# Attention and squared-ReLU MoE kernel: chunk 1's strided heads on TensorE, the first chunk's heads in another order, and gh written by VectorE in chunk 0

## Chip, cores and metric

The kernel runs on one core of one Trainium2 chip. The metric is the device time of one execution in microseconds. Three runs of the kernel before took 883.71 to 884.16 us, the median is 883.96 us. Its engines are named as the profile does: PE (TensorE, matmuls), PEld (its weight loads), DVE (VectorE), ACT (ScalarE), POOL (GpSimd) and SP (SyncE, which issues the DMAs).

## The reference

Attention over 8 batches, 8 heads, 576 positions and head size 64, with two masks: heads 0 to 3 are local (each position sees itself and the 31 before it), heads 4 to 7 are strided (each position sees those before it with the same remainder by 32). The result, as 4608 tokens of 512 features, goes through a feed-forward layer of width 2048 with a squared ReLU.

```python
scores = scale * np.matmul(q, k.transpose(0, 1, 3, 2))
mask_local = (rel >= 0) & (rel < stride)
mask_strided = (rel >= 0) & (pos[None, :] % stride == pos[:, None] % stride)
...
attn = attn / (np.sum(attn, axis=-1, keepdims=True) + 1e-09)
out = np.matmul(attn, v)
...
h = np.maximum(x @ w_in, 0.0)
return (h * h @ w_out).astype(np.float32)
```

## The kernel before

**Chunks and slots.** The tokens are cut into 12 chunks of 384 (`SEGS` names the two pieces of 192 of each). For each chunk, 16 slots j go over the 2048 features, 128 at a time. `up` (L452) makes 12 matmuls of 128x384 into a PSUM tile h: four pieces of x (two local ones, `xlh`/`xll` for their high and low part, two strided ones, `xsh`/`xsl`), each as high x high, high x low and low x high. ScalarE and VectorE then square the ReLU and split it into `gh` and `gl`, and `down` (L480) makes nine matmuls of 128x512 per slot into three y tiles. An up slot of a chunk needs all four pieces of its x.

**Attention.** Where the heads of a chunk are computed depends on the chunk. Chunk 0 takes all its heads through TensorE, in pairs (`pe_pair`, L292): two local pairs (`first`) and two strided pairs (`late`), whose positions are sorted by remainder so that the mask is block-wise. A pair is loaded (q and k in one tile `qk`, v in another), then come scores on TensorE with masked minima on VectorE, exponentials and normalising (factor `rs`), transposes on TensorE with copies to `pt`, and output matmuls, whose results are split into x's high and low part. Chunk 1 takes its local pairs this way too (`local`, L540), in chunk 0's slots. Its strided heads, and those of all later chunks, are computed by `strided` (L387) on GpSimd and VectorE: products per lane on GpSimd (L412 tile `pq`, L434 tile `pp`), each reduced by VectorE (L413, L435). The local heads of chunks 2 to 11 go through `pe_head` (L196).

**The buffers around the seam.** In chunk 1 all matmuls of a pair go to one PSUM bank, number 3, in turn: `pair_at(c, pr, True, pr, "3")`. In chunk 0 each pair has two banks of its own. A pair's SBUF tiles are taken from pools that are used in rotation; the second pair's v and both its score tiles come from the pool of three y output tiles (`ysb`).

**Weights.** They arrive as 64-bit integers' halves and are converted by `convert` (L147): ScalarE scales the raw tile (L154) and makes z (L166), VectorE joins them (L169), ScalarE casts the high part (L172), GpSimd subtracts for the low part (L173). Three of 16 tiles are converted before the first slot, the others in chunk 0's slots.

**The order.** In chunk 0, `up` and `down` of each slot are written one after the other, down two slots behind up. From slot 16 on, slots go in twos: two ups, two downs, with the next chunk's `pe_head` steps between, and each group is fixed behind the one before it. So chunk 1's first two up slots are followed by chunk 0's down slots 14 and 15. Between these fixed groups a scheduler places everything else, by readiness in its own model; `SPREAD` sets how fast the steps for chunk 1 are handed to it in chunk 0's slots (11 slots for the local pairs, 8 for the strided heads). Each engine, SP's DMA issues among them, then works through its queue in the written order.

Of the kernel before, what the change touches and what calls it, by code (L numbers as in the profile page):

```python
# [12 lines left out]
ALU = mybir.AluOpType  # L13
# [28 lines left out]

SPREAD = ((11, 8), (13, 13))

# [42 lines left out]
def attn_moe(ctx: ExitStack, tc, qk_l, v_l, qk_d, v_d, qk_p, v_p, f_s, q_s, k_s, v_s, w_in, w_out, masks, eye, out):  # L87
# [59 lines left out]
    def convert():  # L147

        split = None

        def scale(k):
            for raw, _ in raws[k]:

                nc.scalar.activation(f32(raw[:, :, 1]), f32(raw[:, :, 1]), AF.Prelu, scale=2.0**-112, alpha=-(2.0**32))  # L154

        scale(0)
        for k in range(NFT):
            p, which = order[k]
            t = wpool.tile([P, 2, 1024], F32R, name=f"w{which}_{p}", tag=f"w{k}")
            (wo if which else wi)[p] = t[:, 0], t[:, 1]  # L160
            cuts = [(raw[:, i : i + WP], sl.start + i) for raw, sl in raws.pop(k) for i in range(0, sl.stop - sl.start, WP)]
            for raw, at in cuts:

                z = psum(zbank[next(zturn) % len(zbank)], f"z{k}_{at}").bitcast(U32)
                w, hi, lo = raw[:, :, 1], t[:, 0, at : at + WP], t[:, 1, at : at + WP]
                first_step = nc.scalar.activation(z, raw[:, :, 0], AF.Copy, bias=-0.49, scale=2.0**-29 * (1 - 2.0**-9))  # L166
                if split:
                    split()
                last["v"] = nc.vector.scalar_tensor_tensor(out=w, in0=w, scalar=3, in1=z, op0=ALU.logical_shift_left, op1=ALU.bitwise_or)  # L169

                def split(w=w, hi=hi, lo=lo, at=at, k=k):
                    last["a"] = nc.scalar.copy(hi, f32(w))  # L172
                    last["g"] = nc.gpsimd.tensor_sub(lo, f32(w), f32(hi))  # L173
                    if at and 4 <= k < 12:
                        fetch(k + 4)

                if not at and k + 1 < NFT and k + 1 in raws:
                    with tc.issue_after(first_step.ins):
                        scale(k + 1)
                yield  # L180
        split()
# [110 lines left out]
    def pe_pair(c, pr, local, qk, vr, es, pt, banks, sm, single):  # L292
# [3 lines left out]
        if local:  # L296
            kw, wins, nv = KW, [at for _, _, at in windows(c)], P
            src, vsrc = qk_d[c, pr], v_d[c, pr]
            mk = [mask_sb[:QC, w % 2, :] for w in range(NW)]
        else:  # L300
            kw, wins, nv = QC, [QC * w for w in range(NW)], QC
            src, vsrc = qk_p[pr], v_p[pr]
            mk = [mask_sb[:QC, 3, :QC]] * NW
# [11 lines left out]
        s_ps = [banks() for _ in range(2)] if c == 0 else None  # L315
        e4 = [e[:QC, : NW * kw].rearrange("p (w k) -> p w k", k=kw) for e in es]
        def scores(h, w, s):
# [24 lines left out]
        for h in range(2):  # L342
            if single:
                for w in range(NW):
                    last["a"] = nc.scalar.activation(e4[h][:, w], e4[h][:, w], AF.Exp, bias=nm[:QC, h, w : w + 1], scale=-1.0, accum_out=ss[:QC, NW * h + w, :1])  # L345
            else:
# [5 lines left out]
        for h in range(2):  # L352
            last["g"] = nc.gpsimd.tensor_mul(e4[h], e4[h], rs[:QC, h].unsqueeze(2).broadcast_to([QC, NW, kw]))
        yield
        p4 = pt.rearrange("p (h w q) -> p h w q", h=2, w=NW)
        for h in range(2):
            t = s_ps[h] if s_ps else banks()
            for w in range(NW):
                nc.tensor.transpose(t[:kw, w * QC : (w + 1) * QC], e4[h][:, w], ident[:QC, :QC])  # L359
            last["a"] = nc.scalar.copy(pt[:kw, h * TC : (h + 1) * TC], t[:kw, :TC])  # L360
        yield
        x = x_tiles(c)
        if local:
            o = s_ps[0] if s_ps else banks()
            for w in range(NW):
                for h in range(2):
                    nc.tensor.matmul(o[D * h : D * (h + 1), w * QC : (w + 1) * QC], v4[:kw, h, w], p4[:kw, h, w], start=True, stop=True)
            outs = [(o[:, :TC], [x["l", s][:, pr, :] for s in "hl"])]
        else:

            r0 = D * pr
            outs = []
            for a in range(2):
                o = s_ps[a]
                for w in range(NW):
# [3 lines left out]
                by_i = lambda t: t[r0 : r0 + D].rearrange("p (s i r) -> p s i r", s=2, r=STR)  # L379
                outs.append((o[r0 : r0 + D, :TC].rearrange("p (s r i) -> p s i r", s=2, i=SI), [by_i(x["s", s][:, a, :]) for s in "hl"]))  # L380
        for src, (xh, xl) in outs:
            last["a"] = nc.scalar.copy(xh, src)
            last["v"] = nc.vector.tensor_sub(xl, src, f32(xh))  # L383
        yield
# [67 lines left out]
    def up(c, j):  # L452
# [14 lines left out]
        if c == 0:  # L467

            r = p_t[j % 2].rearrange("p w q -> p (w q)")
            nc.scalar.activation(r, g, AF.Relu)  # L470
            nc.vector.scalar_tensor_tensor(out=g, in0=g, scalar=0.0, in1=r, op0=ALU.max, op1=ALU.mult)
# [3 lines left out]
        last["gh"] = nc.scalar.copy(gh, g)  # L475
        nc.vector.tensor_sub(gl, g, f32(gh))  # L476
# [126 lines left out]
    with tc.issue_after(last["p"].ins):  # L603
        zeros(0, NWARM // 2)
        for k in range(NEARLY, 8):
            fetch(k)
    next(late[0])
    with tc.issue_after(last["p"].ins):
        zeros(1, NWARM // 2)
    next(first[0])  # L610
    next(first[1])
    weights = behind({"a": last["a"]}, ungated)
    next(late[1])
    for i in range(2):
        next(first[0])
        next(first[1])
        next(late[0])
        next(late[1])
        if i:
            weights = behind({"a": last["a"]}, ungated)  # L620
        for _ in range(2):
            next(weights)
    next(late[0])
    next(late[1])
    for _ in range(2 * NEARLY - 4):
        next(weights)
# [4 lines left out]
    for s in range(NS + 2):  # L631
# [29 lines left out]
        if c + 1 < NCHUNK and s >= LATER:  # L661
            j0 = LATER if c == 0 else 0
            if j == j0:
                lo, st = local(c + 1) if c == 0 else iter(()), strided(c + 1)
                if c == 0:
                    lo, st = behind(heads_end, lo), behind(heads_end, st)
                if c == 1:
# [19 lines left out]
def _layout(q, k, v, moe_w_in, moe_w_out):  # L687
# [21 lines left out]

    by_r = lambda t: rows(t[:, HL:], 0).reshape(HL, 2, SI, STR, D).transpose(0, 1, 3, 2, 4).reshape(HL, TC, D)  # L710
    a["qk_p"] = asc(np.concatenate([by_r(t).transpose(0, 2, 1) for t in (q, k)], axis=2)).reshape(2, P, 2 * TC)
    a["v_p"] = two(by_r(v).reshape(HL, NW, QC, D).transpose(0, 2, 1, 3).reshape(1, HL, QC, NW * D)).reshape(2, QC, 2 * NW * D)

# [44 lines left out]
```

## Time and profile before

| what | value |
|---|---|
| median of three runs | 883.96 us |
| the profiled execution | 883.18 us |
| its span, first to last instruction | 881.4 us |
| mean granted TensorE clock | 0.997 |
| VectorE, ScalarE, GpSimd busy | 72%, 65%, 77% |
| TensorE, PEld busy | 99%, 90% |

Columns of the profile's rows: in a timeline, start, length, engine, line, operation, output<-input, shape and count, and in brackets the idle time before and what ended it. In the chain of work that ended last, start, length, engine, tile and line; each row there is work, or a wait, that nothing else hides. In groups, the busy time of all, the mean length of one in ns, and the idle time before them with what ended it. In the table of stretches, from:to, length, busy time of each engine with its number of instructions, then the granted clock (1.00 is full), the DMA engines' busy share and GB/s. Lengths of neighbouring instructions can overlap, and one fp32 matmul counts as two records. In DMA rows, the size, and the median time from issue to landing.

### The profile page before, as it was taken

What the parts mean: (1) busy time and instruction counts of PE and PEld (TensorE: products, weight loads), DVE (VectorE), ACT (ScalarE), POOL (GpSimd) and SP (SyncE); (2) the same over time, 40 slices, a digit from 0 to 9 for tenths busy, and PEclk for the clock granted to TensorE, in tenths of its full rate; (3) what the DMA queues carried; (4) which work ended last, traced back from release to release, by engine and by line L of the source; (5) the groups of instructions that cost most, each with busy time, mean ns of one, the idle gap of its engine ahead of it and who ended that gap; (6) DMA issues with size and microseconds to landing.
All of it is one profiled execution on the core that took longest, in us unless ns stands there. A gap on an engine that the chain in (4) does not pass through costs nothing.

```text
span 881.4 us, 14862 instructions
## 1 busy us (share of the span) xinstructions
PE 868.5 (99%) x4744; PEld 789.6 (90%) x4744; DVE 635.5 (72%) x1892; ACT 572.6 (65%) x1510; POOL 676.8 (77%) x722
## 2 busy tenths in 40 slices
PE   8899999999999999999999999999999999999997
PEld 7788899999999999999999999999999989998996
DVE  4578687788777888878778778778787787883111
ACT  6798776676676666757657747657666665664332
POOL 4698878878978989898988978997898899782000
PEclk9999999999999999999999999999999999999999
DMA  9851631323123123104102302312131121000000
GB/s 356 355 195 63 184 121 42 103 84 113 32 66 112 37 89 103 44 30 127 44 13 80 115 14 74 104 31 74 31 102 57 30 71 61 7 1 10 28 1 36
DMA packets 26798, 71.41 MB, mean 81 GB/s; under 512 B 2976, under 2 KB 8736, under 8 KB 25184
## 3 DMA queue, kind: packets, MB, share of 16 engines
q1 hardware_dynamic: 26432, 70.14, 23.9%
q8 instruction: 37, 0.61, 0.3%
q10 hardware_dynamic: 288, 0.33, 0.1%
q14 instruction: 41, 0.34, 0.1%
HBM read 61.01 MB, written 9.44 MB: 80 GB/s over the span
## 4 chain that ended last, share of the span: by engine, by line
PE 95%; ACT 3%; DVE 1%; POOL 0%; issue 0%; DVEq 0%; POOLq 0%; ACTq 0%
PE h L462 44%; PE y L489 44%; PE s L234 2%; PE o L280 2%; ACT e L345 1%; PE w_ps L586 1%; ACT raw L154 1%; PE b L319 1%; DVE sc L419 0%; ACT z L166 0%; ACT w L172 0%; DVE raw L169 0%; ACT pt L360 0%; PE b L359 0%; DVE xsl L383 0%
## 5 line engine op out<-in xcount | busy, mean ns | idle before, releaser
L489 PE MATMUL y<-w,gh 128*128 128x512 f32 x1152 | 357.1, 391 | 0.8 <-ACT gh L475 0.8
L489 PEld LDWEIGHTS y<-w,gh 128*128 128x128 f32 x1152 | 212.5, 188 | 41.5 <-ACT gh L475 1.4
L462 PE MATMUL h<-xlh,w 128*128 128x384 f32 x768 | 229.6, 339 | 2.1 <-DVE xsl L383 1.6
L462 PE MATMUL h<-xsh,w 128*128 128x384 f32 x768 | 226.2, 335 | 0.0
L489 PE MATMUL y<-w,gl 128*128 128x512 f32 x576 | 224.0, 392 | 0.0
L434 POOL TENSOR_TENSOR pp<-vs,sc 128x448 f32<-128x448 f32 (+10 forms) x192 | 189.8, 1014 | 39.8 <-DVE qs L435 18.2
L412 POOL TENSOR_TENSOR pq<-ks,qs 128x512 f32<-128x512 f32 (+2 forms) x192 | 197.8, 1050 | 17.9 <-DVE sc L413 13.8
L476 DVE TENSOR_TENSOR gl<-h,gh 128x384 fp32r<-128x384 f32 x192 | 105.4, 550 | 84.2 <-ACT gh L475 82.9
L475 ACT CAST gh<-h 128x384 fp32r<-128x384 f32 x192 | 91.4, 477 | 103.0 <-PE y L489 100.0
L473 ACT ACTIVATE h<-h 128x384 f32<-128x384 f32 x176 | 83.0, 472 | 107.8 <-PE h L462 106.2
L413 DVE TENSOR_REDUCE sc<-pq 128x8 f32<-128x512 f32 (+4 forms) x228 | 119.6, 534 | 46.2 <-POOL pq L412 43.9
L462 PEld LDWEIGHTS h<-xlh,w 128*128 128x128 f32 x768 | 142.1, 188 | 5.6 <-DVE xsl L383 1.8
L462 PEld LDWEIGHTS h<-xsh,w 128*128 128x128 f32 x768 | 141.7, 188 | 0.3
L462 PE MATMUL h<-xll,w 128*128 128x384 f32 x384 | 129.3, 337 | 0.0
L435 DVE TENSOR_REDUCE qs<-pp 128x64 f32<-128x448 f32 (+11 forms) x192 | 106.7, 563 | 31.0 <-POOL pp L434 29.5
L489 PEld LDWEIGHTS y<-w,gl 128*128 128x128 f32 x576 | 108.1, 188 | 22.9
L462 PE MATMUL h<-xsl,w 128*128 128x384 f32 x384 | 128.5, 335 | 0.0
L474 ACT ACTIVATE h<-h 128x384 f32<-128x384 f32 x176 | 83.2, 473 | 3.6
L259 DVE STREAM_TRANSPOSE p_t<-e 32x128 f32<-32x128 f32 x240 | 72.3, 301 | 10.4 <-ACT e L248 6.0
L462 PEld LDWEIGHTS h<-xll,w 128*128 128x128 f32 x384 | 72.5, 189 | 2.2
L462 PEld LDWEIGHTS h<-xsl,w 128*128 128x128 f32 x384 | 72.2, 188 | 0.0
L243 ACT ACTIVATE e<-e,nm 96x128 f32<-96x128 f32 x160 | 62.5, 392 | 10.5 <-DVE nm L226 8.8
(97 smaller groups left out, 1077.2 us busy)
## 6 DMA issues: line engine op xcount, KB each, us to landing
qk<-qk_l SPq DMA_DIRECT2D x24, 400.0 KB, 3.2
y<-ysb SPq DMA_DIRECT2D x36, 256.0 KB, 3.7
raw<-w_in SPq DMA_DIRECT2D x7, 1024.0 KB, 11.2
qk<-qk_l SPq DMA_DIRECT2D x16, 416.0 KB, 3.3
vs<-v_s SPq DMA_DIRECT2D x10, 576.0 KB, 4.0
raw<-w_out SPq DMA_DIRECT2D x5, 1024.0 KB, 12.9
v<-v_l SPq DMA_DIRECT2D x40, 128.0 KB, 2.0
ks<-k_s SPq DMA_DIRECT2D x8, 576.0 KB, 3.8
```

The costliest lines, as they stand in the source:

```text
L243: nc.scalar.activation(e[:QC, cut(w)], e[:QC, cut(w)], AF.Exp, bias=nmax[:QC, w : w + 1], scale=-1.0, accum_out=ssum[:QC, w, :1])
L259: nc.vector.transpose(out=pt[STR * k : STR * (k + 1), :, STR * r : STR * (r + 1)], in_=e.rearrange("p (w k) -> p w k", k=KW)[STR * r : STR ...
L412: nc.gpsimd.tensor_mul(pv, kt[:, a : a + m, :], qt[:, i - i0 : i - i0 + 1, :].broadcast_to([P, m, D]))
L413: nc.vector.tensor_reduce(out=sc[:, i - i0, a : a + m], in_=pv, op=ALU.add, axis=AX.X)
L434: nc.gpsimd.tensor_mul(pv, vt[:, a : a + nd, :n], sc[:, il : il + 1, :n].broadcast_to([P, nd, n]))
L435: nc.vector.tensor_reduce(out=ot[:, il, a : a + nd], in_=pv, op=ALU.add, axis=AX.X)
L462: done = nc.tensor.matmul(ph[:, :TC], w[:, wsl], xx, start=n == 0, stop=n == 11)
L473: nc.scalar.activation(g, g, AF.Relu)
L474: nc.scalar.activation(g, g, AF.Square)
L475: last["gh"] = nc.scalar.copy(gh, g)
L476: nc.vector.tensor_sub(gl, g, f32(gh))
L489: done = nc.tensor.matmul(y_ps[c][t], g[:, sl], w[:, wsl], start=j == 0 and k == 0, stop=j == NFT - 1 and k == 2)
```

## The change

There are four parts.

1. **Chunk 1's strided heads** are computed by `pe_pair` on TensorE. `pairs` takes the place of `local`: after the ten steps of the two local pairs come ten steps of two strided pairs, in the same bank 3 and from the same pools, handed out over 12 slots. `strided` begins with chunk 2. The host lays out `qk_p` and `v_p` for two chunks.
2. **The first chunk's heads.** In the local pairs of chunk 0 the exponentials are written to the PSUM tile of the scores, and VectorE multiplies them with `rs` into SBUF, where GpSimd did it in place. The copies of the strided pairs' transposes to `pt` go from ScalarE to VectorE. Each output's cast and subtraction follow its matmuls at once. The steps are written in another order; 20 warm-up matmuls take the place of two times 30, and the first weight tile's second half is split at once.
3. **In chunk 0's slots** the ReLU is written twice by ScalarE, VectorE writes the product once to `gh` and once to PSUM, and ScalarE's cast to `gh` goes.
4. **`SPREAD`** becomes `((12, 8), (13, 13))`, with 20 steps where there were 10.

```diff
-SPREAD = ((11, 8), (13, 13))
+SPREAD = ((12, 8), (13, 13))
...
+                if k == 0 and at:
+                    split()
+                    split = None
...
+        r4 = [blocks(t) for t in s_ps] if single else e4
...
-                    last["a"] = nc.scalar.activation(e4[h][:, w], e4[h][:, w], AF.Exp, bias=nm[:QC, h, w : w + 1], scale=-1.0, accum_out=ss[:QC, NW * h + w, :1])
+                    last["a"] = nc.scalar.activation(r4[h][:, w], e4[h][:, w], AF.Exp, bias=nm[:QC, h, w : w + 1], scale=-1.0, accum_out=ss[:QC, NW * h + w, :1])
...
-            last["g"] = nc.gpsimd.tensor_mul(e4[h], e4[h], rs[:QC, h].unsqueeze(2).broadcast_to([QC, NW, kw]))
+            eng, key = (nc.vector, "v") if single else (nc.gpsimd, "g")
+            last[key] = eng.tensor_mul(e4[h], r4[h], rs[:QC, h].unsqueeze(2).broadcast_to([QC, NW, kw]))
...
-            last["a"] = nc.scalar.copy(pt[:kw, h * TC : (h + 1) * TC], t[:kw, :TC])
+            (nc.vector.tensor_copy if c == 0 and not local else nc.scalar.copy)(pt[:kw, h * TC : (h + 1) * TC], t[:kw, :TC])
...
+        def parts(src, dst):
+            last["a"] = nc.scalar.copy(dst[0], src)
+            last["v"] = nc.vector.tensor_sub(dst[1], src, f32(dst[0]))
...
-                o = s_ps[a]
+                o = s_ps[a] if s_ps else banks()
...
             nc.scalar.activation(r, g, AF.Relu)
-            nc.vector.scalar_tensor_tensor(out=g, in0=g, scalar=0.0, in1=r, op0=ALU.max, op1=ALU.mult)
+            last["gh"] = nc.scalar.activation(r, g, AF.Relu)
+            for t in (gh, g):
+                nc.vector.scalar_tensor_tensor(out=t, in0=g, scalar=0.0, in1=r, op0=ALU.max, op1=ALU.mult)
...
-    def local(c):
-        heads = [pair_at(c, pr, True, pr, "3") for pr in range(2)]
-        for h in (0, 0, 1, 0, 1, 0, 0, 1, 1, 1):
-            next(heads[h])
-            yield
+    def pairs(c):
+        for kind in (True, False):
+            heads = [pair_at(c, pr, kind, pr, "3") for pr in range(2)]
+            for h in (0, 0, 1, 0, 1, 0, 0, 1, 1, 1):
+                next(heads[h])
+                yield
...
-                lo, st = local(c + 1) if c == 0 else iter(()), strided(c + 1)
...
+                lo, st = (behind(heads_end, pairs(c + 1)), iter(())) if c == 0 else (iter(()), strided(c + 1))
...
-            while dl < fl * 10 and next(lo, "end") != "end":
+            while dl < fl * 20 and next(lo, "end") != "end":
```

What this does to the written order shows at the seam between chunk 0 and chunk 1. The first engine is TensorE. Before, chunk 0's down slot 13 (the rows with y) is followed by chunk 1's first up slot, h_0; the names xl are local pieces of x, xs strided ones.

```order
L489 MATMUL y_2_614<-w_6_1218,gl_13_1307 128x512
L462 MATMUL h_0_1397<-xlh_901,w_0_413 128x384
L462 MATMUL h_0_1397<-xll_902,w_0_413 128x384
L462 MATMUL h_0_1397<-xlh_901,w_0_413 128x384 x2
L462 MATMUL h_0_1397<-xll_902,w_0_413 128x384
L462 MATMUL h_0_1397<-xlh_901,w_0_413 128x384
L462 MATMUL h_0_1397<-xsh_903,w_0_413 128x384
```

Now, at the same place and behind three matmuls each for h_0 and h_1, stand the last steps of local pair 1 (b_1_1: transposes L366, outputs L379) and then the scores of the strided pairs (L325; b_0_0 is pair 0, b_1_0 is pair 1).

```order
L366 MATMUL b_1_1_926<-ident,e_1_1_651 128x96 x4
L379 MATMUL b_1_1_978<-pt_1_1_652,v_1_1_649 64x96 x8
L470 MATMUL h_0_1408<-xlh_850,w_0_372 128x384
L470 MATMUL h_1_1427<-xlh_850,w_0_372 128x384
L325 MATMUL b_0_0_1049<-qk_0_0_1035 96x96 x4
L470 MATMUL h_0_1408<-xll_851,w_0_372 128x384
L470 MATMUL h_0_1408<-xlh_850,w_0_372 128x384
L470 MATMUL h_1_1427<-xll_851,w_0_372 128x384
L470 MATMUL h_1_1427<-xlh_850,w_0_372 128x384
L325 MATMUL b_0_0_1058<-qk_0_0_1035 96x96 x4
L325 MATMUL b_1_0_1165<-qk_1_0_1040 96x96 x4
L325 MATMUL b_1_0_1174<-qk_1_0_1040 96x96 x4
```

Right behind these come the strided pairs' transposes (L366) and outputs (L389), and the rest of h_0 and h_1, which reads xs.

```order
L366 MATMUL b_0_0_1223<-ident,e_0_0_1037 96x96 x4
L366 MATMUL b_0_0_1229<-ident,e_0_0_1038 96x96 x4
L389 MATMUL b_0_0_1235<-pt_0_0_1039,v_0_0_1036 32x96 x8
L389 MATMUL b_0_0_1246<-pt_0_0_1039,v_0_0_1036 32x96 x8
L366 MATMUL b_1_0_1298<-ident,e_1_0_1042 96x96 x4
L366 MATMUL b_1_0_1304<-ident,e_1_0_1043 96x96 x4
L389 MATMUL b_1_0_1355<-pt_1_0_1044,v_1_0_1041 32x96 x8
L470 MATMUL h_0_1408<-xsh_852,w_0_372 128x384
L470 MATMUL h_1_1427<-xsh_852,w_0_372 128x384
L389 MATMUL b_1_0_1366<-pt_1_0_1044,v_1_0_1041 32x96 x8
```

So all of the strided pairs' matmuls have come to stand between two parts of chunk 1's first two up slots.

The second engine is SP, with its DMA issues for the same place. Before, the loads for chunk 2's strided heads (qkvs_4 and the rows with 6) follow the last weight tiles (raw).

```order
L144 DMA raw_512_1099<-w_out 128x1024
L392 DMA qkvs_4_1492<-f_s 128x1152
L399 DMA qs_6_1651<-q_s 128x384
L400 DMA ks_6_1652<-k_s 128x768
L401 DMA vs_6_1653<-v_s 128x1152
L211 DMA qk_2_1626<-qk_l 128x832
```

Now the strided pairs' v stand between them; v_1_0 goes into the buffer of v_1_1, which the outputs b_1_1_978 above read.

```order
L144 DMA raw_512_1025<-w_out 128x1024
L311 DMA v_0_0_1036<-v_p 96x512
L311 DMA v_1_0_1041<-v_p 96x512
L215 DMA v_0_1340<-v_l 128x256
L215 DMA v_1_1345<-v_l 128x256
L400 DMA qkvs_4_1503<-f_s 128x1152
L407 DMA qs_6_1662<-q_s 128x384
```

The load of qkvs_4 has moved behind the load of v_1_0, and so behind those outputs.

The third is VectorE. Before, the subtraction that makes xll of local pair 1 (L383) stands ahead of the first reductions for chunk 2 (L413, sc_4).

```order
L383 TENSOR_TENSOR xll_902<-b_1_1_1282,xlh_901 128x384
L169 SCALAR_TENSOR_TENSOR raw_512_1099<-raw_512_1099,z_512_1277 128x512
L471 SCALAR_TENSOR_TENSOR h_14_1323<-h_14_1323,p_t_90 128x384
L413 TENSOR_REDUCE sc_4_1494<-pq_4_0_0_1496 128x1
L471 SCALAR_TENSOR_TENSOR h_15_1367<-h_15_1367,p_t_91 128x384
L413 TENSOR_REDUCE sc_4_1494<-pq_4_1_0_1499 128x2
```

Now it stands behind three of them (L421), and the first minima of a strided pair (L330) behind five.

```order
L486 TENSOR_TENSOR gl_15_1391<-h_15_1377,gh_15_1390 128x384
L421 TENSOR_REDUCE sc_4_1505<-pq_4_0_0_1507 128x1
L421 TENSOR_REDUCE sc_4_1505<-pq_4_1_0_1510 128x2
L421 TENSOR_REDUCE sc_4_1505<-pq_4_2_0_1513 128x3
L373 TENSOR_TENSOR xll_851<-b_1_1_978,xlh_850 128x384
L421 TENSOR_REDUCE sc_4_1505<-pq_4_3_0_1516 128x4
L421 TENSOR_REDUCE sc_4_1505<-pq_4_4_0_1519 128x5
L330 ISA e_0_0_1037,nm_0_0_1047<-b_0_0_1049,mask_sb 96x96
```

The subtraction that frees bank 3 has moved behind reductions of products that GpSimd makes from qkvs_4. On GpSimd, four operations stand between the second strided pair's first subtraction (L353 in the new numbering) and the first product with `rs` (L360): two products `pp`, then kx and qx of chunk 2's first local head.

More of the change, by code (lines that the diff above doesn't have):

```diff
@@ L379, in pe_pair @@
                 by_i = lambda t: t[r0 : r0 + D].rearrange("p (s i r) -> p s i r", s=2, r=STR)
[L380 to L383, printed above, removed]
+                parts(o[r0 : r0 + D, :TC].rearrange("p (s r i) -> p s i r", s=2, i=SI), [by_i(x["s", s][:, a, :]) for s in "hl"])
         yield
@@ L607, in attn_moe @@
     next(late[0])
-    with tc.issue_after(last["p"].ins):
-        zeros(1, NWARM // 2)
+    zeros(1, NWARM // 3)
+    next(first[0])
+    parts = last["v"], last["a"]
+    with tc.issue_after(parts[1].ins):
+        next(first[1])
+    weights = behind({"a": last["a"]}, ungated)
+    with tc.issue_after(parts[0].ins):
+        next(late[1])
     next(first[0])
     next(first[1])
-    weights = behind({"a": last["a"]}, ungated)
+    next(late[0])
     next(late[1])
-    for i in range(2):
-        next(first[0])
-        next(first[1])
+    for _ in range(2):
+        next(weights)
+    next(first[0])
+    next(first[1])
+    for _ in range(2):
         next(late[0])
         next(late[1])
[L619 to L625, printed above, removed]
+    weights = behind({"a": last["a"]}, ungated)
+    for _ in range(2 * NEARLY - 2):
         next(weights)
```

19 lines of the change are left out of this document (8 added, 11 removed).

## The prediction

> **What bounds the kernel now.** The page first, for which engine carries the time, and its chain that ended last:
>
> ```profile
> PE 868.5 (99%) x4744; PEld 789.6 (90%) x4744; DVE 635.5 (72%) x1892; ACT 572.6 (65%) x1510; POOL 676.8 (77%) x722
> PEclk9999999999999999999999999999999999999999
> PE 95%; ACT 3%; DVE 1%; POOL 0%; issue 0%; DVEq 0%; POOLq 0%; ACTq 0%
> ```
>
> TensorE is 95% of the chain. A busy TensorE is not yet a full one, so the next view is the chain in order of time. It shows the first up matmuls of two neighbouring chunks:
>
> ```profile
> 131.85 4.19 PE h L462 x24
> 201.91 4.19 PE h L462 x24
> ```
>
> ```profile
> 220.00:440.00 220.00, 220.00 (x1158) 201.38 (x1157) 175.49 (x521) 145.89 (x404) 193.73 (x202) 1.00 0.22 69
> ```
>
> A chunk lasts 201.91 - 131.85 = 70.06 us, and the stretch of 220 us has TensorE busy throughout, the first number behind the comma. So from chunk 1 on nothing can be caught up: what is lost before chunk 1's up matmuls stays lost, and what is won there stays won. Only chunk 0 and the seam to chunk 1 need working out. The first of the next rows is from the timeline of TensorE, the others are the chain's:
>
> ```profile
> 30.44 0.69 PE L462 MATMUL h<-xlh,w 128*128 128x384 f32 x1 [1.61 <-DVE xsl L383]
> 39.17 2.34 PE y L489 x9
> 45.69 4.18 PE h L462 x24
> 49.88 4.12 PE y L489 x18
> 54.35 1.04 PE b L319 x8
> 75.99 0.35 PE b L359 x4
> 98.76 0.81 PE b L367 x16
> 105.31 2.11 PE h L462 x12
> 107.43 2.36 PE h L462 x12
> 109.78 0.47 PE s L234 x4
> ```
>
> Chunk 0's first up matmul starts at 30.44, chunk 1's at 105.31, and chunk 1's first two up slots are through at 109.78: 4.5 us for 24 matmuls, without a hole. The prices: an up slot 4.18 / 2 = 2.09, a down slot 4.12 / 2 = 2.06; of a local pair the scores of one head 1.04, its transposes 0.35, the pair's outputs 0.81. Between 30.44 and 105.31 stand 16 up slots (33.4), 14 down slots (28.8) and the local pairs (4 x 1.04 + 4 x 0.35 + 2 x 0.81 = 7.2): 69.4 of 74.9 us. The loss is 5.5 us.
>
> **TensorE's new work.** Chunk 1's strided pairs bring 16 score matmuls of 96 columns: 4 heads x 1.04 x 96 / 128 = 3.1 us; four groups of transposes, 4 x 0.35 = 1.4; and 32 output matmuls (two row groups per pair, 8 each), priced like the local pair's 8: 4 x 0.81 = 3.2. Together 7.7 us. TensorE has no idle time in which to hide them, and loses no matmul of its own for them but warm-up ones. The work on VectorE and GpSimd that goes was off the chain, but for a part of the 5.5 us.
>
> **The start.** ScalarE carried it. These are rows of the chain, and one of GpSimd's timeline:
>
> ```profile
> 8.76 6.27 ACT e L345 x32
> 16.52 0.36 ACT pt L360
> 27.27 0.54 ACT z L166
> 28.41 1.05 ACT raw L154
> 29.46 0.36 ACT xsh L382
> 12.60 2.03 POOL L353 TENSOR_TENSOR e<-e,rs 96x512 f32<-96x512 f32 x2 [9.74 <-DVE rs L351]
> 25.05 0.47 ACT L360 COPY w<-b 96x384 f32<-96x384 f32 x1 [1.56 <-PE b L359]
> ```
>
> Between 8.76 and the last xsh cast, ScalarE now leaves out the third raw scaling (1.05), one z (0.54) and the four strided pt copies, which go to VectorE (4 x 0.36 = 1.44): 3.0 us. The normalising of the local heads goes from GpSimd (2.03 for two) to VectorE, and GpSimd reaches the strided heads' products (L353) earlier; that takes up to the 1.56 of idle time before the copy at 25.05. The exponentials write to PSUM, each waiting for the one before it in its bank: up to half a microsecond back. Bounds 2.5 to 4.6, since the copies cost VectorE some 0.5 each between other things; I take 3.7, nearest to the sum of the removed rows plus half the wait. First up matmul at 26.7. The 40 warm-up matmuls fewer lay in TensorE's idle time.
>
> **Chunk 0's slots.** The groups of the slots' own operations:
>
> ```profile
> L475 ACT CAST gh<-h 128x384 fp32r<-128x384 f32 x192 | 91.4, 477 | 103.0 <-PE y L489 100.0
> L470 ACT ACTIVATE p_t<-h 128x384 f32<-128x384 f32 x16 | 7.7, 492 | 1.8 <-PE h L462 1.8
> L471 DVE SCALAR_TENSOR_TENSOR h<-h,p_t 128x384 f32<-128x384 f32 x16 | 9.0, 561 | 4.6 <-ACT p_t L470 4.5
> ```
>
> ScalarE wins nothing: the second Relu stands where the cast to gh stood, 0.49 for 0.48. VectorE gets 16 more products of 0.56, 9 us in 70, and loses chunk 1's reductions; it has the room. The loss of 5.5 us is kept as it was, between 3 (the products' wait at 38 us goes) and 7.5 (an earlier start meets the same ScalarE, which is the next engine to be late, since it converts the weights). Before the seam stand 69.4 less the last transposes and outputs of local pair 1 (1.2): chunk 1's first up matmul starts at 26.7 + 68.2 + 5.5 = 100.4, that is 4.9 earlier than now.
>
> **The seam.** Here the written order of the queues decides. TensorE runs six l matmuls of h_0 and h_1, the last transposes and outputs of local pair 1, and then every matmul of the strided pairs; what is left of h_0 and h_1 is strewn between, and the down slots 14 and 15 stand behind. All steps share PSUM bank 3, so each waits until ScalarE or VectorE has read the one before. The rows for it, from the DMA view, the timelines and the groups by form:
>
> ```profile
> 0.74 0.85 SPq L305 DMA_DIRECT2D qk<-qk_d  x2
> vs<-v_s SPq DMA_DIRECT2D x10, 576.0 KB, 4.0
> qkvs<-f_s SPq DMA_DIRECT2D x6, 576.0 KB, 5.2
> 37.05 3.81 POOL L412 TENSOR_TENSOR pq<-qkvs 128x64 f32<-128x64 f32 x6
> 14.60 0.82 POOL L347 TENSOR_TENSOR e<-e,nm 96x384 f32<-96x384 f32 x1
> 14.10 0.25 DVE L324 CUSTOM_DVE_ANT_0 e<-b,mask_sb 96x96 f32<-96x96 f32 x1
> 14.28 0.25 DVE L324 CUSTOM_DVE_ANT_0 e<-b,mask_sb 96x96 f32<-96x96 f32 x1
> L218 POOL TENSOR_TENSOR kx<-qk,kx 128x448 fp32r<-128x448 f32 x16 | 18.5, 1156 | 7.2 <-ACT kx L217 6.2 <-POOL xll L288 1.0
> L220 POOL TENSOR_TENSOR qx<-qk,qx 64x384 fp32r<-64x384 f32 x40 | 40.5, 1013 | 3.1
> L360 ACT COPY pt<-b 96x384 f32<-96x384 f32 x2 | 0.9, 475 | 0.0
> L383 DVE TENSOR_TENSOR xsl<-b,xsh 64x384 fp32r<-64x384 f32 x4 | 2.1, 553 | 3.8 <-ACT xsh L382 3.8
> ```
>
> With S for the start of chunk 1's up matmuls, step by step. Six matmuls (1.05), transposes (0.35), copy (0.48), outputs (0.81), each with a little to be signalled: local pair 1 is out at S + 2.9. SyncE has been waiting for just that, because the load of v_1_0 goes into the buffer that these outputs read, and queued behind it are two loads of v and the load of qkvs_4. Three issues of 0.85 / 2 come before it, and it lands after 4.0 to 5.2 us; I take 4.0, as the queues are then empty: S + 8.2. GpSimd's products of qkvs_4 and VectorE's reductions of them stand ahead of VectorE's subtraction for xll, which frees bank 3; three of the six products (3.81 for all) with their reductions make 1.7, the subtraction 0.55: the first strided scores start at S + 10.5.
>
> Then four rounds of scores (0.78) and minima (4 x 0.18 = 0.72). The third round's minima are ready some 5 us later, the rounds and the reductions between them counted. Behind them GpSimd has a subtraction (0.82), two small products (0.73), kx (1.16), qx (1.01) and only then the first product with rs (0.82), 4.5 in all: the first transposes start at S + 20.
>
> The rest is a chain. Per pair: transposes, copy, transposes, copy (2 x 0.83), and two times outputs, cast and subtraction (2 x 1.84), with ten signals of about 0.05: 5.9; two pairs 11.8. VectorE's subtractions stand behind reductions that wait for GpSimd, some 2 us more, by the products queued there. The up slots are through at S + 34, where it was S + 4.5. **The seam costs 29.5 us**, 7.7 of them matmuls. Its floor, with every queue empty, would be the outputs, four rounds and two pair chains, 2.9 + 6.6 + 11.8 = S + 21; its ceiling, with the DMA at 5.2 and each signal twice as long, S + 38.
>
> **The clock.** These stretches are from the start, where TensorE also waits between bursts:
>
> ```profile
> 26.00:30.00 4.00, 2.56 (x46) 1.85 (x40) 1.40 (x3) 3.48 (x7) 1.30 (x1) 1.00 1.00 417
> 30.00:32.00 2.00, 1.56 (x5) 1.56 (x6) 1.94 (x4) 1.90 (x4) 0.00 (x1) 0.53 0.98 397
> 32.00:34.00 2.00, 2.00 (x9) 2.00 (x8) 0.86 (x2) 1.79 (x3) 1.78 (x2) 0.62 1.02 406
> ```
>
> After a stretch with 2.56 of 4 us busy the granted clock falls to 0.53 and 0.62 for 4 us: 1.7 us lost. In the seam TensorE has about 12 us of work in 31, and is idle from S + 3.7, behind two more l matmuls, to S + 10.5. Bounds: nothing, or all 7.7 at half the clock and 1.7 to come back, 9.4. I take 4: it falls, and part of it is hidden under GpSimd.
>
> The Trainium skill, "TensorE: Matmul & The Clock Gate", "What's actually happening", puts the gate at half rate after an idle window of about 3.4 us and back only after a busy one as long. By that rule the wait for the load halves the clock and no burst in the seam restores it, so the sum would have 9.4 here; the 0.53 agrees with the rate, but shows no such idle window.
>
> **The sum.** -4.9 + 29.5 + 4 = +28.6 us. The profiled execution is 883.18 (span 881.4 and 1.8 around it), the median of the runs 883.96; the sum is made against the first, 911.8, and 0.8 is added: 912.6.
>
> **The rivals.** *Half the clock all through the seam*: 9.4 for 4 gives 918. For it: the idle stretch; against it: 26 to 30 us, at the full clock in short bursts. Chance 0.25.
>
> *The order looks worse than it is*, the chains' steps are ready when TensorE comes, and only the matmuls remain: 883.96 - 4.9 + 7.7 = 887. For it: in the trace of before the local pairs' steps, in the same bank, cost no visible hole. Against it: those have slots of other matmuls between them, these have none. Chance 0.06.
>
> *Faster*: the start wins more than the matmuls cost. It decides from the point where the first up matmul starts before 24 us, nothing waits at the seam and the loss in the slots falls from 5.5 to 3: 883.96 - 6.5 - 2.5 + 7.7 = 882.7, and a microsecond earlier still passes the bound. For it: ScalarE is busy almost without a hole before 30 us; against it: 16 exponentials alone take it to 15 us, and the written order puts the seam's waits where no start reaches. Chance 0.02. As much for a time within 0.2%, which is 1.8 us and about what a measurement of this kernel can tell from no change. That the strided vector work stays is excluded: the reductions for batches 2 and 3 are gone from VectorE's queue.
>
> **The numbers.** The forecast has 0.65, slower in all 0.96. The range, 898 to 924: below, the seam at S + 22 with no loss of clock and the start as taken (883.96 - 4.9 + 17.5 = 897), above, a seam at S + 38, half the clock and a start 1 us worse (922). It leaves out the two last rivals and the mere matmuls, 0.1, and as much again for mistakes of mine in the chain.
>
> **What would show it.** Right: the first up matmul near 27 us; a hole of 5 to 8 us on TensorE right after the outputs of local pair 1, ended by VectorE's subtraction, with the qkvs load landing in it; then some twelve short bursts with holes ended by VectorE, ScalarE and GpSimd; chunk 1's second up slot through at 130 to 145; 70.06 per chunk after it. Wrong: that slot through before 120, or chunks longer than before.

## The result and the profile after

| | before | after |
|---|---|---|
| median, lowest to highest | 883.84 us (883.00 to 884.16, 4 runs) | 913.97 us (912.14 to 915.96, 4 runs) |
| the profiled execution, its span | 883.18, 881.4 us | 915.96, 914.2 us |
| mean granted TensorE clock | 0.997 | 0.974 |

The ratio is 1.0343, 95% interval 1.0321 to 1.0365: 30.1 us slower by the medians, 32.8 in the profiled executions. On the page of after, TensorE is still nearly the whole chain, but the clock row has holes where it had none.

```profile
PE 887.6 (97%) x4816; PEld 803.9 (88%) x4816; DVE 643.0 (70%) x1920; ACT 575.4 (63%) x1514; POOL 661.7 (72%) x698
PEclk8799958999999999999999999999999999999999
PE 94%; ACT 2%; POOL 1%; DMA 1%; DVE 1%; issue 0%; SPq 0%; DVEq 0%; POOLq 0%; ACTq 0%
```

A slice is 22.9 us: the first five digits cover the start and chunk 0, the 5 covers 114 to 137 us. The timeline of TensorE gives the start and the seam step by step (in brackets the idle time ahead of a row, and what ended it).

```profile
18.27 1.54 PE L379 MATMUL b<-pt,v 128*64 128x96 f32 x14 [1.58 <-ACT pt L367]
...
30.29 0.44 PE L470 MATMUL h<-xlh,w 128*128 128x384 f32 x1
...
104.48 0.33 PE L470 MATMUL h<-xlh,w 128*128 128x384 f32 x1
...
106.60 0.88 PE L379 MATMUL b<-pt,v 128*64 128x96 f32 x16 [0.57 <-ACT pt L367]
108.06 0.62 PE L470 MATMUL h<-xlh,w 128*128 128x384 f32 x2 [0.58 <-ACT xlh L372]
110.84 1.15 PE L325 MATMUL b<-qk 64*96 64x96 f32 x8 [2.16 <-DVE xll L373]
...
118.45 1.59 PE L325 MATMUL b<-qk 64*96 64x96 f32 x8 [0.89 <-DVE nm L330]
123.12 0.87 PE L366 MATMUL b<-ident,e 96*96 96x96 f32 x4 [3.08 <-POOL e L360]
...
126.06 1.50 PE L389 MATMUL b<-pt,v 96*32 96x96 f32 x16 [0.56 <-ACT pt L367]
...
131.66 0.85 PE L366 MATMUL b<-ident,e 96*96 96x96 f32 x4 [1.45 <-POOL pq L420]
```

The first up matmul starts at 30.29, hardly earlier than before (30.44). Chunk 1's first one starts at 104.48; in the same view of before that was 105.14 (the chain's 105.31 counts from the end of the matmul ahead). Then come the twelve short bursts that were expected, nearly all behind a wait, and nearly all long: scores 1.59, transposes 0.87 and outputs 1.50, where the same view has 0.92 (experiment 2), 0.51 and 0.85 (experiment 3, second try) at the full clock. The chain of after shows what filled the first hole, the end of the seam, and the period behind it.

```profile
103.06 5.52 DMA qkvs<-f_s
...
108.65 1.29 POOL pq L420 x3
...
110.32 0.47 DVE xll L373
...
139.13 3.32 PE h L470 x10
142.45 0.46 PE s L237 x4
...
147.03 4.19 PE h L470 x24
...
217.10 4.19 PE h L470 x24
```

Chunk 1's first two up slots are through at 142.45, 32.7 later than before (109.78): that is the whole difference of 32.8. A chunk behind it lasts 217.10 - 147.03 = 70.07, as before (70.06). The table of stretches shows the clock (behind the busy times: granted clock, DMA share, GB/s). First a stretch from the start of before:

```profile
20.00:22.00 2.00, 1.40 (x19) 1.08 (x20) 1.25 (x2) 2.00 (x6) 1.40 (x2) 1.00 1.03 426
```

Then stretches of after, from the start and from the seam:

```profile
20.00:22.00 2.00, 2.00 (x14) 2.00 (x14) 1.51 (x6) 2.00 (x4) 1.26 (x2) 0.50 1.00 418
...
28.00:29.00 1.00, 1.00 (x24) 1.00 (x21) 0.55 (x1) 0.37 (x1) 0.00 (x0) 0.50 0.97 393
...
108.00:111.00 3.00, 0.78 (x4) 0.46 (x5) 1.54 (x5) 0.01 (x1) 2.35 (x5) 1.00 1.02 417
111.00:123.00 12.00, 7.27 (x36) 5.93 (x35) 7.60 (x48) 2.67 (x6) 7.33 (x10) 0.52 0.24 79
...
131.00:142.00 11.00, 8.49 (x51) 6.84 (x52) 5.06 (x11) 1.93 (x5) 8.18 (x10) 0.50 0.10 30
```

The seam ran at half the clock from 111 to 142 (123 to 131, not shown, has 0.50 too), and so did the start from 16 to 29 us, where before had 1.00.

### The profile page after: what moved, and what is told of

It is laid out like the page before. It is cut to its first block, busy times and chain, and to the rows that moved or that the text cites. A ratio compares the mean times of both kernels' runs of the same rounds, so it can differ in the third digit from the quotient of the medians.

```text
span 914.2 us, 15024 instructions
## 1 busy us (share of the span) xinstructions
PE 887.6 (97%) x4816; PEld 803.9 (88%) x4816; DVE 643.0 (70%) x1920; ACT 575.4 (63%) x1514; POOL 661.7 (72%) x698
## 3 DMA queue, kind: packets, MB, share of 16 engines
q1 hardware_dynamic: 26656, 70.14, 22.9%
## 4 chain that ended last, share of the span: by engine, by line
PE 94%; ACT 2%; POOL 1%; DMA 1%; DVE 1%; issue 0%; SPq 0%; DVEq 0%; POOLq 0%; ACTq 0%
PE h L470 43%; PE y L499 43%; PE s L237 2%; PE o L283 2%; PE b L325 1%; PE b L389 1%; PE b L366 1%; ACT b L351 1%; DMA qkvs<-f_s 1%; PE w_ps L597 1%; PE b L379 0%; POOL pq L420 0%; ACT raw L154 0%; POOL e L360 0%; POOL pp L442 0%
## 5 line engine op out<-in xcount | busy, mean ns | idle before, releaser
L420 POOL TENSOR_TENSOR pq<-ks,qs 128x512 f32<-128x512 f32 (+2 forms) x192 | 197.7, 1049 | 27.9 <-DVE sc L421 22.7
L421 DVE TENSOR_REDUCE sc<-pq 128x8 f32<-128x512 f32 (+3 forms) x216 | 115.4, 543 | 52.2 <-POOL pq L420 49.0
L485 ACT CAST gh<-h 128x384 fp32r<-128x384 f32 x176 | 83.9, 476 | 96.9 <-PE y L499 95.6
L246 ACT ACTIVATE e<-e,nm 96x128 f32<-96x128 f32 x160 | 62.5, 392 | 14.3 <-DVE nm L229 13.9
```

Of the source, the lines that this page charges most:

```text
L246: nc.scalar.activation(e[:QC, cut(w)], e[:QC, cut(w)], AF.Exp, bias=nmax[:QC, w : w + 1], scale=-1.0, accum_out=ssum[:QC, w, :1])
L420: nc.gpsimd.tensor_mul(pv, kt[:, a : a + m, :], qt[:, i - i0 : i - i0 + 1, :].broadcast_to([P, m, D]))
L421: nc.vector.tensor_reduce(out=sc[:, i - i0, a : a + m], in_=pv, op=ALU.add, axis=AX.X)
```

## The experiments

The theory after this reading, A: the seam is a chain of steps that nothing covers, made longer by the half clock and by chunk 2's work in the queues; the start's gain went to the half clock too. The rivals name other causes. Each result is also given as the median's distance from the kernel before, run beside it on the same chip; the changed kernel is at +30.1. Most kernels were run four times, and the medians of so few can move by a microsecond or two; where a trace says more, it is named.

**1. More warm-up matmuls.**

```diff
-    zeros(1, NWARM // 3)
+    zeros(1, NWARM - 10)
```

> The changed kernel with 50 warm-up matmuls in the start where it has 20. Theory A (the start's gain of 3.7 us was eaten by TensorE at half the clock from 16 us on, because fewer warm-up matmuls left it idle from 12.1 to 14.1): the clock stays at 1.00 until the slots, the first up matmul starts at 25 to 27 in place of 30.3, and the kernel takes 909.5 to 912.5, some 3 less than the 914 of the changed kernel. Rival B (VectorE, ScalarE and GpSimd set the pace of the start whatever the clock): the first up matmul stays at 29.5 or later and the time at 913 to 915.

Measured: 914.17 us, +29.9 (ratio 1.034, 1.031 to 1.037). The test missed its own condition. The stretch of it in which TensorE waited (the clock is the third number from the end):

```profile
16.00:18.00 2.00, 0.17 (x3) 0.00 (x0) 2.00 (x16) 2.00 (x7) 1.53 (x2) 0.58 1.06 434
```

Its timeline of TensorE around it:

```profile
18.13 1.92 PE L379 MATMUL b<-pt,v 128*64 128x96 f32 x16 [1.96 <-ACT pt L367]
...
33.16 0.69 PE L470 MATMUL h<-xlh,w 128*128 128x384 f32 x1
```

The added matmuls were through at 12.7, TensorE waited 1.96 us for ScalarE all the same, and the clock fell as that wait began (0.79 from 16.2 to 16.4, 0.50 behind it), so the wait itself can't be the whole cause. The up matmuls began even later. It tells nothing between A and B, only that 30 more matmuls in front don't hold the clock up in this start.

**2. Chunk 2's products behind the pairs.**

```diff
+                if c == 0:
+                    pairs_end = {e: last[e] for e in "agsv"}
...
-                    st = behind(weights_end, st)
+                    st = behind(pairs_end, st)
```

> The changed kernel with chunk 2's strided products, their reductions and their loads placed behind the pairs of chunk 1 on every engine. Theory A (GpSimd's and VectorE's queue order costs the seam what the chain shows: 2.2 us before the first strided scores, 0.7 before the first transposes, about 1.5 between the two pairs' outputs): 909 to 911, 3 to 5 less than the changed kernel. Rival B (the one PSUM bank and TensorE's bursts set the pace, the products fit beside them): within 1 us of 914.

Measured: 912.48 us, +28.2 (1.0323, 1.0306 to 1.034): 1.9 less than the changed kernel where A had 3 to 5 and B less than 1. Its chain at the seam:

```profile
104.75 1.06 PE h L470 x6
...
111.51 3.25 DMA qk<-qk_l
...
137.88 0.85 PE s L237 x4
```

Its timeline of TensorE, first scores and first transposes:

```profile
108.76 0.92 PE L325 MATMUL b<-qk 64*96 64x96 f32 x8
...
118.58 0.88 PE L366 MATMUL b<-ident,e 96*96 96x96 f32 x4 [3.49 <-POOL e L360]
```

The hole before the first scores is gone, the scores run at the full clock (0.92), and in this execution the seam ends at 137.88, 4.6 earlier. Another wait stands in the place of a part of it: GpSimd's kx for chunk 2's local heads waits for its load (3.25), and the products with rs stand behind it. The two traced executions both have a late first up matmul (30.29 and 31.09), and as a whole they are 3.7 us apart, inside A's window; the changed kernel's median is lower than its traced execution, since two of its four runs took 912.14 and 912.53. So the queue order costs 2 us by the medians and 3.7 to 4.6 by the traces.

**3. The seam filled**, in the kernel of experiment 2. Small matmuls on the mask tile into bank 4, whose results are not read, behind the steps of the strided pairs; the pairs' steps are handed out over 18 slots, which leaves their place in TensorE's order as it is.

```diff
-SPREAD = ((12, 8), (13, 13))
+SPREAD = ((18, 8), (13, 13))
...
+        def fill(n):
+            if c == 1 and (pr == 1 or not local):
+                t = psum(4, f"fill{u}_{next(tick)}")
+                idle = mask_sb.rearrange("p a b -> p (a b)").bitcast(BF16)[:, :P]
+                with tc.issue_after(last["p"].ins):
+                    for _ in range(n):
+                        nc.tensor.matmul(t[:, :P], idle, idle, start=True, stop=True)
...
+                if not local:
+                    fill(14 if pr == 0 or h == 0 else 30)
...
```

> The same with 10 to 30 small matmuls on constant data into a free bank behind every step of the strided pairs in the seam, so that TensorE is hardly idle there. Theory A (the half clock in the seam costs what the bursts are longer: 4 scores by 0.8, 4 transposes by 0.4, 4 outputs by 0.65 and the up matmuls by 1.6, in all 9 us, little of it hidden): granted clock 1.00 through the seam and 6 to 8.5 us less than the kernel with the products behind. Rival B (the waits for VectorE, ScalarE and GpSimd hide the longer bursts, as the prediction took for part of it): at most 3 us less, or more time for the added matmuls.

Measured: 909.83 us, +25.6 (1.0279, 1.0254 to 1.0305), 2.6 less than experiment 2: between the theories. The fills got in the way themselves: a weight conversion that shares bank 4 came between the first and the second scores, and the clock still fell behind 120 (0.87 from 120 to 122, 0.50 from 122 to 124). So a second try filled only from the last scores on, with 52, 10 and 12 matmuls.

> The kernel with the products behind, and small matmuls into a free bank only from the last strided scores on: 52 behind these, 10 behind each group of transposes, 12 behind each group of outputs. Theory A (half the clock costs the pair chains what it lengthens): granted clock 1.00 through the seam, 15 to 16 us from the first strided transposes to the end of chunk 1's second up slot (19.3 in the kernel with the products behind), and 907.5 to 909.5 in all. Rival B (the waits for the other engines hide it): 911 or more.

Measured: 908.53 us, +24.5 (1.0261, 1.0234 to 1.0288), 3.7 less than experiment 2, as A had it. Its chain behind the last scores:

```profile
116.75 4.63 PE fill L322 x52
121.38 0.33 PE b L378 x4
...
133.49 1.82 PE h L484 x10
135.31 0.47 PE s L237 x4
```

A stretch of it from the pair chains:

```profile
124.00:128.00 4.00, 3.15 (x54) 2.54 (x49) 1.10 (x2) 1.25 (x3) 1.58 (x5) 1.00 0.00 0
```

From the first transposes to the end of the up slots it takes 135.31 - 121.38 = 13.9 us at the full clock, where experiment 2 took 137.88 - 118.58 = 19.3 at half of it, with the same order on TensorE. Rival B falls for this part: the waits hide little. Of the 5.4, some 2 are lost again ahead of it, since the clock had fallen at 113 and the 52 matmuls, run at half of it until then, outlast the wait. The six runs spread from 903.13 to 909.20, so the 3.7 is good to a microsecond or two.

**4. The start filled.** 18 matmuls before and 44 behind the first pair's transposes, into free columns of a bank that is held anyway.

```diff
+        spare[c, pr, local] = s_ps
...
+    def more(n):
+        t = spare[0, 0, False][1]
+        with tc.issue_after(last["p"].ins):
+            for _ in range(n):
+                nc.tensor.matmul(t[:, TC:], warm, warm, start=True, stop=True)
...
+    more(18)
     next(first[0])
+    more(44)
```

> The changed kernel with 18 small matmuls before the transposes of the first local pair and 44 behind them, into free columns of a bank that a strided pair of chunk 0 holds, so that TensorE is busy from 12 to 18 us. Theory A: granted clock 1.00 from 8 to 30 us, first up matmul at 25 to 27 (30.3 without), 2 to 4 us less than the changed kernel, so 910 to 912 for the median where that has 914. Rival B (VectorE, ScalarE and GpSimd set the pace): first up matmul at 29 or later, 913 or more.

Measured: 911.52 us, +27.9 (1.0314, 1.03 to 1.0328): 2.2 to 2.5 less than the changed kernel. The stretch that was idle:

```profile
16.00:18.00 2.00, 1.81 (x33) 1.63 (x31) 2.00 (x10) 2.00 (x6) 1.47 (x3) 1.00 1.07 438
```

The first up matmul in its timeline:

```profile
27.73 0.44 PE L471 MATMUL h<-xlh,w 128*128 128x384 f32 x1
```

The clock holds and the up matmuls start 2.6 earlier: A, though 0.7 later than its window.

**5. The kernel before with fewer warm-up matmuls.** 20 for its two times 30.

> The kernel before with 20 warm-up matmuls behind its first 60 where it has two times 30, all else unchanged. Theory A (warm-up matmuls keep the clock up through the start, and a start at half the clock costs several us): the granted clock falls to 0.5 between 15 and 18 us, the first up matmul starts 1 to 4 us later than 30.44, and the kernel takes 885.5 to 889. Rival B (the other engines set the pace of the start): the clock may fall, but the time stays within 1 us of the kernel before.

Measured: 884.87 us, +1.25 (1.0012, 1.0002 to 1.0021), between the theories. In its profiled execution the clock was down from 15 to 21 us and the first up matmul still came at 29.02, so no cost of the half clock shows there: ScalarE carries that start up to 21.7, as the prediction's chain of before has it, and by then the clock was back. The reading is that not the number of warm-up matmuls costs, but a low clock that lasts into the time when TensorE is the chain, as in after from 18.27 to 30.39.

**6. Where the strided pairs stand.** Once handed out sooner in the one bank, once with two banks as well.

```diff
-SPREAD = ((12, 8), (13, 13))
+SPREAD = ((6, 8), (13, 13))
...
-            heads = [pair_at(c, pr, kind, pr, "3") for pr in range(2)]
+            heads = [pair_at(c, pr, kind, pr, "34") for pr in range(2)]
```

> The changed kernel with all steps of the pairs handed out over 6 slots in place of 12, still in the one bank 3. Theory A (the bank, not the rate of handing out, puts the strided pairs into the seam): their place in TensorE's order is the same, and the time 911 to 917. Rival E (the rate does it): under 905.

Measured, first line alone: 914.39 us, +30.8 (1.035, 1.0321 to 1.0379). Handing out sooner does nothing, and TensorE's order at the seam is the same.

> The changed kernel with the pairs of chunk 1 alternating between PSUM banks 3 and 4, and all their steps handed out over 6 slots in place of 12, by which the strided pairs' steps stand before chunk 1's first up matmul in TensorE's order. Theory A (one bank gives one step per slot, so 12 of 22 steps are left for the seam, where no slot covers them): no hole at the seam, the clock stays up there, and only the added matmuls remain: 888 to 893. Rival D (the same steps cost as much inside the slots, since ScalarE and GpSimd fall behind with the weights): 898 or more.

Measured, both lines: 916.44 us, +32.8 (1.0374, 1.0356 to 1.0391). A fails here. The strided steps do stand in the slots, but two stretches of it show that nothing is won:

```profile
60.00:90.00 30.00, 26.85 (x165) 22.23 (x164) 16.15 (x48) 18.25 (x33) 15.51 (x14) 0.94 0.32 113
90.00:131.00 41.00, 30.53 (x176) 24.83 (x175) 19.52 (x64) 24.44 (x46) 16.90 (x17) 0.75 0.18 56
```

The end of its chain in chunk 0:

```profile
121.60 1.14 ACT raw L154 x2
...
123.88 7.24 PE y L499 x18
```

TensorE is idle for 13.6 of these 71 us, at a clock down to 0.75, and the chain of work runs through ScalarE's weight steps, which are still under way at 122 (the last z starts at 134.2, in after at 94.0). So the weights come late. The second bank is the one in which their z is made; whether that sharing or the number of steps does it was not taken apart. A bank of their own wasn't tried, so rival D stands.

**7. Chunk 1's strided heads back on the vector engines**, the rest of the change kept, their steps handed out as before; then the same with the start filled as in 4.

```diff
-        for kind in (True, False):
+        for kind in (True,):
...
-                lo, st = (behind(heads_end, pairs(c + 1)), iter(())) if c == 0 else (iter(()), strided(c + 1))
+                lo, st = (behind(heads_end, pairs(c + 1)), behind(heads_end, strided(c + 1))) if c == 0 else (iter(()), strided(c + 1))
```

> The changed kernel with chunk 1's strided heads on GpSimd and VectorE as before; the rearranged start and the writing of gh by VectorE stay. Prediction on record: chunk 1 starts 4.9 us earlier and nothing is lost at the seam, 879. As the trace of the changed kernel reads (first up matmul only 0.15 earlier, chunk 1 only 0.8 earlier): 883, no more than 1 us faster than the kernel before. Rival C (GpSimd and VectorE now cannot deliver chunk 1's strided heads in time beside the added products): 885 or more.

Measured: 882.18 us, -2.1, ratio 0.999 (0.9972 to 1.0007): no difference that holds. So it is the strided pairs on TensorE that cost the 30 us: without them no loss is left.

> Chunk 1's strided heads on GpSimd and VectorE as before, the rest of the change kept, and the start filled with 18 and 44 small matmuls. Theory A (the start's gain is there once the clock stays up): first up matmul at 27.5 to 28.5 and 879 to 881, faster than the kernel before by 3 to 5. Rival C (with the start earlier, GpSimd delivers chunk 1's strided heads no earlier, since its wait already ends last there without the fill): 881.5 to 884.

Measured: 887.19 us, +3.2 (1.0039, 1.0024 to 1.0054), more than any theory had. The chain of u2's seam:

```profile
107.76 1.00 POOL xsl L455
...
108.81 3.57 PE h L471 x10
```

GpSimd's last step of the strided heads releases TensorE at 108.8: rival C's wait. The clock falls in it (0.50 from 108 to 112), and C had not priced that. No version here beats the kernel before by a difference that holds.

**8. Only gh by VectorE**, put into the kernel before.

> The kernel before with only the third part of the change: in chunk 0 the ReLU written twice by ScalarE and gh by VectorE. Prediction on record: ScalarE wins nothing, VectorE has the room, so 883 to 885. Rival: VectorE, which then has about 9 us more in chunk 0 beside chunk 1's reductions, is late for the down slots: 886 or more.

Measured: 886.19 us, +2.15 (1.0024, 1.0012 to 1.0036): the rival's side. Its chain ends chunk 0 on GpSimd too:

```profile
110.80 0.98 POOL xsl L446
...
111.82 2.03 PE h L462 x10
```

That VectorE's added products delay GpSimd's strided work through the reductions fits this, but is argued, not shown; the start of this execution ran at half the clock as well (0.50 from 19 to 30), though it has all of the warm-up matmuls of before. If it is so, these 2 us are no part of the changed kernel's loss, since that GpSimd work is gone there.

**9. All three mendings together**: 4, 2 and the late fill of 3.

> The changed kernel with all three: the start filled, chunk 2's products behind the pairs, and the seam filled from the last strided scores on. Theory A (what is then left is the chain of the strided pairs itself, at the full clock): 904 to 907, still 20 or more slower than the kernel before. Rival B (the three overlap, and the seam loses elsewhere what it wins): 909 or more.

Measured: 905.72 us, +21.7 (1.0245, 1.0223 to 1.0267), as A had it. Its chain:

```profile
102.27 1.06 PE h L485 x6
...
109.03 3.27 DMA qk<-qk_l
...
131.63 0.47 PE s L237 x4
```

Chunk 1's up matmuls start 3.0 before the kernel before (105.31 in the same view), and the seam lasts 131.63 - 102.27 = 29.4 where that had 4.5: 24.9 - 3.0 = 21.9, near the measured 21.7. So of the 30.1 us the three mendings take 8.4. By the medians of the single ones these are about 2.3 for the half clock in the start, 2 for the products in the queue and 3.7 for the half clock in the seam. What is left, near 22, is a seam 24.9 longer, less the 3.0 by which chunk 1 now starts earlier. Not all of that seam need be the pairs' own: from 109.03 to 115.25 its chain goes through the load, kx and qx of chunk 2's first local head, which stand ahead of the products with rs. How much of these 6.2 us would go with them moved was not run.

## Why the prediction was right, point by point

- **Place and mechanism** were right: everything is lost at the seam, in a chain of bursts behind waits, and the period of a chunk stays 70.07. The seam's end, S + 34 with 4 for the clock, is S + 38.0 in the trace (142.45 - 104.48). That it fits so well is luck: the way to the first scores was put 4.1 too long, and what follows it took 8.1 more than was said for it, where 4 was taken for the clock.
- **The first scores**: S + 10.5 was said, S + 6.4 came (110.84). The step that failed is that the load of v_1_0 goes into the buffer that local pair 1's outputs read. The waits of SP's queue say otherwise:

```profile
SPq L311 <- PE b L366: 7.2, 1, 7.2
SPq L311 <- PE b L379: 5.4, 1, 5.4
```

  One v load waited for outputs (those of pair 0, at 94), the other for transposes (L366), those at 101.3, and not for the outputs at 106.60. The view names no buffers, but the tile that these transposes free is the score tile of pair 1's first head, which comes from the same pool as the v tile. SyncE was free 2.8 us before S. The hole was 2.16, not 5 to 8. Part of the gain went to the landing: the qkvs load took 5.52 and not 4.0. The queues were not empty, since SyncE let eight loads go between 101.69 and 106 (DMA share 0.92 from 104 to 108); that this made it longer fits, but was not tested.
- **The first transposes**: S + 20 was said, S + 18.6 came. From the first scores it took 12.3, not 9.5, at half the clock.
- **The pair chains**: 14 was said: two of 5.9, and 2 for products queued in between. 13.9 was measured at the full clock (experiment 3), 19.3 in after. The two chains hold, but the rest is luck. The products cost next to nothing here, as it is 19.3 with them (after) and without (experiment 2). In their place stand the ten matmuls of h_0 and h_1 behind the last outputs, which the working left out: 1.82 at the full clock, 3.32 in after.
- **The clock in the seam**: 4 was taken, between 0 and 9.4. The fills won 3.7 by the medians and 5.4 in the chains alone. With up to 2.8 more ahead of these (12.3 for 9.5), an estimate from these numbers is 5 to 8, between what was taken and the rival's 9.4. And the clock in after is the rival's: half nearly through the whole seam. The argument against it, the start's full clock in short bursts, did not carry over. The page "TensorE: Matmul & The Clock Gate" of the Trainium skill, section "What's actually happening", has the clock come back after a busy window of about 3.4 us. Between 115.1 and 136.7 no burst of the seam is that long, and the 0.50 agrees; but from 110.84 to 115.1 TensorE was busy for 4.2 without a hole, and the clock stayed down.
- **The start**: 3.7 was said, 0.15 came in the profiled execution. The step that failed is that TensorE would not matter in the start, its idle time being free: the clock fell in it, and TensorE itself became the chain from 18.27 to 30.39. That the 40 warm-up matmuls left out made it fall is not shown, since it also fell with 30 of them back (experiment 1) and in the start of before with all of them (experiment 8). With the start filled it wins 2.7 (27.73). In the trace of experiment 6's first kernel, which has the same start in the same order, the clock came back sooner, and the first up matmul started at 26.49, the forecast's 26.7. Its chunk 1 starts at 99.80, where the prediction has 100.4, its seam ends at 137.75, S + 38.0 again, and that execution took 911.24, where the forecast has 911.8. So the 4.7 us between it and the traced execution of after lie all ahead of S. Its timeline of TensorE, without a hole from the first of these rows until the clock was back:

```profile
17.64 1.54 PE L379 MATMUL b<-pt,v 128*64 128x96 f32 x14 [1.57 <-ACT pt L367]
...
26.49 0.44 PE L470 MATMUL h<-xlh,w 128*128 128x384 f32 x1
...
99.80 0.33 PE L470 MATMUL h<-xlh,w 128*128 128x384 f32 x1
```

Two stretches of it, between which the clock came back:

```profile
20.00:21.00 1.00, 1.00 (x9) 1.00 (x8) 0.57 (x2) 1.00 (x4) 0.88 (x2) 0.50 1.01 418
...
22.00:23.00 1.00, 1.00 (x9) 0.64 (x8) 0.98 (x3) 0.85 (x2) 1.00 (x2) 1.00 1.05 434
```

- **Chunk 0's slots**: 5.5 kept. From first up matmul to S it took 74.2 where 73.7 was said: right within 0.5. By itself the new writing of gh costs about 2 in the kernel before (2.15, interval 1.1 to 3.2), which was not foreseen.
- **The sum**: 28.6 said, 30.1 by the medians, 32.8 in the profiled execution. In that one the seam came out by luck, and what is missing is the start. The upper bound's terms make 923, not the 922 that was written; it changes nothing.

## What to carry to other kernels

Before moving work onto a full engine, look for where its steps will stand: seven microseconds of matmuls cost thirty, most of it because their chain of copies and waits had no other matmuls beside it. In the slots, sharing a bank with the weights, they cost as much, so whether any place would have hidden them is open. Idle time of TensorE isn't always free to make longer: here the clock that it lost was paid by the work that followed, 5.4 of 19.3 us in the pair chains. When a load waits for a buffer, find which instruction frees that buffer in the trace, not from the order in which tiles were asked for.

## What was not expected of the hardware

The clock fell without a long idle stretch: in after the longest single wait ahead of the fall was 2.01 us in the start and 2.16 in the seam, each with shorter ones around it, and in experiment 1 it was 0.76, with the next wait only just begun. The page "TensorE: Matmul & The Clock Gate" of the Trainium skill, section "What's actually happening", has it fall after an idle window of about 3.4 us and come back after a busy one as long; one kernel's start agrees with the second half (busy from 17.64, back between 21 and 22) and another, with the same order on TensorE, does not (busy from 18.27, still 0.50 from 28 to 29). That start is a likely reason for the two levels in which the changed kernel's runs lie: 912.14 and 912.53 with a mean granted clock of 0.977, 915.41 and 915.96 with 0.974. The two kernels' traces, 911.24 and 915.96, differ ahead of S alone, which fits. A trace of each level of one kernel wasn't taken, so it stays open.
